# Raw weight words: the sign carried through the rebias by a leaky ReLU, and a new order of all work

## The chip, the cores and the metric

The kernel runs on one core of one Trainium2 chip. The metric is device time of one execution in microseconds (us), lower is better; a kernel's time is the median of its runs. The engines are called as in the profile: PE (matrix multiply; PEld is its weight load), DVE (vector), ACT (activations), POOL (general purpose) and SP (which issues the DMAs).

## The reference

Windowed attention (8 x 8 heads, 576 tokens, head size 64, window 64), whose result for all 4608 tokens goes through a gated feed-forward network with weights 512 x 2048 and 2048 x 512:

```python
scores = where(0 <= i - j < 64, q @ k.T / 8, -1e9)
attn   = softmax(scores)
x      = (attn @ v), heads side by side        # 4608 x 512
h      = x @ w_in                              # 4608 x 2048
g      = h * erf(softplus(h))
out    = g @ w_out                             # 4608 x 512
```

q, k and v are float32. The two weight matrices are drawn as float64, so that each weight reaches the kernel as two 32-bit words, a low and a high one.

## The kernel before, in words

**Attention.** Tokens are cut into 36 units of 128 (number u), two units to a chunk of 256 (number c, 18 chunks). Each unit's q, k and v are loaded (`lq`, `lk`, `lv`), their largest magnitudes found (`pk`) and turned into powers of two per chunk (`pa`, `pb`, `px`, `py`, `pc`). Every operand of a matrix product is split into two float16 parts, a high one (`qh`, `kh`, `vh`) and a rest (`ql`, `kl`, `vl`), and each product is three matmuls. Scores (`s`), masked maximum (`m`), shift (`f`), two exponentials (`e`), the rest of the weights (`r`), a transposing DMA (`t`), the weighing of v (`a`), normalization (`n`), the split of the result (`xh`, `xl`) and another transposing DMA into `xt` (`xt`) follow.

**Feed-forward.** A group g (36 of them) is one chunk with one half of the 2048 hidden columns. Its first product, `mm:g:0` to `mm:g:3` (24 matmuls each, PSUM tiles hp0 and hp1 in turn), needs `xt` of the chunk and both parts of `w_in`. Each piece is taken out of PSUM by an eviction `ev` on DVE or ACT into `h`; softplus (`sp`) and erf (`er`) run on ACT for half a group at a time, DVE multiplies (`gt`), `gh` and `gl` make the float16 parts, and `mA` (16 matmuls of 512 columns) and `mB` (8) form the second product in PSUM tiles o0 and o1, from where `fo` moves it to the result and `st` stores it. ACT holds one table of functions at a time: exponentials, softplus and erf each need their own, and the build puts an ACT_TABLE_LOAD wherever the next activation needs another one than the last.

**Weights.** They come in 16 units of 1 MB (`L`), eight of `w_in`, then eight of `w_out`, into six slots that are reused (`SLOTS`). A unit is 128 x 1024 pairs of words. For each unit the double is turned into a float32 in place: the high word, read as a float32, is multiplied by 2^-112 (`rebias`, token `c`); it is shifted left by 3 and joined with the low word's top three bits (`assemble`, token `o`, DVE). The shift pushes the sign out, so the sign is kept apart. Either `sign_plane` (token `g`, ACT or POOL) writes it into a tile `plane` and `low_bits` (`d`, DVE) joins the shifted low word with it, or `low_bits2` (`dd`, two DVE instructions) takes it from the high word. Then `b` (`bound`) finds the largest magnitude, `mb`, `mx`, `my`, `mc` make the scale of a pair of units, `h` writes the float16 high part, and `lp` on PE with `le` the rest (for two units `l` on DVE). `wm` tokens are matmuls on an identity whose result nobody reads; they run where PE has nothing else.

**Order.** `PLAN` is a list of 2356 tokens, written out in the file; each token calls the function of its name, and instructions stand on every engine's queue in the order of the tokens. The last letter names the engine (v DVE, a ACT, g POOL). Each engine works through its queue in order.

Of the kernel before, what the change touches and what calls it, by code (L numbers as in the profile page):

```python
# [8 lines left out]
F32 = mybir.dt.float32  # L9
# [28 lines left out]
SIGN = -(2 ** 31)  # L38
# [175 lines left out]
def window_attention_gated_ffn(ctx, tc, q, k, v, w_in, w_out, masks, out):  # L214
# [82 lines left out]
    for t in planes:  # L297
        nc.gpsimd.memset(t, 0)
# [185 lines left out]
    def low_bits(u):  # L484
        lo = raw(u)[0]
        nc.vector.scalar_tensor_tensor(lo, lo, 29, planes[u % len(planes)], op0=ALU.logical_shift_right, op1=ALU.bitwise_or)
# [225 lines left out]
```

## Time and profile before

| | |
|---|---|
| runs | 932.92 us median of 3 (929.71 to 935.45) |
| profiled execution | span 929.5 us, first to last instruction; no time of its own is given beside the span |
| PE | busy 897.9 us (97% of the span) |
| DVE | busy 714.7 us (77%) |
| ACT | busy 634.4 us (68%), in it 116 table loads |
| POOL | busy 290.8 us (31%) |
| DMA | 98.63 MB, mean 106 GB/s |

"Busy" of PE includes the `wm` matmuls. A group of instructions in the profile has a line (of the kernel), an engine, an operation, tiles written and read, a count, busy time and the mean of one in ns. Idle time is put down to what ended it.

### The profile page before, as it was taken

How to read it: one execution, taken by the hardware profiler on the slowest of the kernel's cores; microseconds unless marked ns; L12 is line 12 of the kernel's file. 1: busy time of each engine (PE TensorE's matmuls, PEld its weight loads, DVE VectorE, ACT ScalarE, POOL GpSimd, SP SyncE). 2: the span in 40 equal slices, each digit the busy share in tenths (PEclk: the TensorE clock that was granted, in tenths of full speed). 3: DMA queues.
4: the chain of work that ended last, by engine and by line, in shares of the span. 5: the costliest groups of instructions: out<-in, count | busy, mean ns of one | idle time of the engine just before them, and what ended most of it. 6: DMA issues, size and time to landing. Idle time of an engine off the chain costs nothing.

```text
span 929.5 us, 22240 instructions
## 1 busy us (share of the span) xinstructions
PE 897.9 (97%) x9281; PEld 603.5 (65%) x9281; DVE 714.7 (77%) x1506; ACT 634.4 (68%) x749; POOL 290.8 (31%) x299
## 2 busy tenths in 40 slices
PE   8779998999999999999999999999999999999998
PEld 8546566656766666667666767566667566766663
DVE  6989887988888998785976876986876976845443
ACT  4888976888675886959764758764768764924333
POOL 1343333425244353441330541330541430501000
PEclk9989999999999999999999999999999999999999
DMA  9585747144443555445353525352625250301000
GB/s 366 171 199 182 202 86 197 41 96 132 112 129 81 114 128 124 84 111 102 93 86 102 113 88 103 92 92 102 112 84 103 91 105 33 70 23 24 24 23 23
DMA packets 140532, 98.63 MB, mean 106 GB/s; under 512 B 117776, under 2 KB 117904, under 8 KB 140432
## 3 DMA queue, kind: packets, MB, share of 16 engines
q1 hardware_dynamic: 140432, 97.22, 42.2%
q8 instruction: 72, 1.18, 0.5%
q14 instruction: 28, 0.23, 0.1%
HBM read 59.44 MB, written 9.44 MB: 74 GB/s over the span
## 4 chain that ended last, share of the span: by engine, by line
PE 79%; DVE 10%; DMA 5%; ACT 3%; issue 1%; POOL 1%; DVEq 0%; POOLq 0%; ACTq 0%
PE hp L590 36%; PE o L626 35%; PE av L427 3%; PE s L394 2%; DMA vr<-v_in 2%; PE o L553 1%; DMA stage<-w_out 1%; DVE y L610 1%; DMA qr<-q_in 1%; DVE gl L322 1%; DMA xt<-xs 1%; DMA stage<-w_in 1%; DVE vs L322 1%; DVE sm L403 1%; DVE stage L504 1%
## 5 line engine op out<-in xcount | busy, mean ns | idle before, releaser
L590 PE MATMUL hp<-xt,w 128*128 128x256 f16 x3456 | 401.8, 274 | 7.8 <-DMA xt<-xs 3.6
L590 PEld LDWEIGHTS <-w 128*128 128x128 f16 x3456 | 336.7, 98 | 70.4 <-issue 11.4
L626 PE MATMUL o<-w,gh 128*128 128x512 f16 x1152 | 260.9, 379 | 2.5 <-DVE w L444 1.8
L626 PEld LDWEIGHTS <-gh 128*128 128x128 f16 x1152 | 110.3, 98 | 125.8 <-issue 2.4
L317 DVE TENSOR_SCALAR h<-hp,c 128x512 f32<-128x512 f32 x123 | 90.9, 745 | 79.4 <-PE hp L590 79.0
L626 PE MATMUL o<-w,gl 128*128 128x512 f16 x576 | 136.4, 380 | 0.0
L602 ACT ACTIVATE y<-h 128x1024 f32<-128x1024 f32 x72 | 73.6, 1052 | 91.3 <-DVE h L317 90.1
L408 POOL TENSOR_TENSOR sm<-sm,mx 128x512 f32<-128x512 f32 x66 | 71.7, 1099 | 105.8 <-DVE mx L403 105.5
L322 DVE SCALAR_TENSOR_TENSOR gl<-y,sg,gh 128x1024 f16<-128x1024 f32 x72 | 97.4, 1354 | 5.8 <-PE o L626 4.0
L610 DVE TENSOR_TENSOR y<-h,y 128x1024 f32<-128x1024 f32 x72 | 95.3, 1333 | 8.4 <-ACT y L606 8.2
L626 PEld LDWEIGHTS <-gl 128*128 128x128 f16 x576 | 54.1, 98 | 56.3 <-DVE gl L322 0.5
L450 POOL TENSOR_TENSOR xs<-x,xs 128x512 f16<-128x512 f32 x32 | 46.5, 1453 | 140.3 <-ACT xs L442 107.8
L606 ACT ACTIVATE y<-y 128x1024 f32<-128x1024 f32 x72 | 73.7, 1050 | 0.5
L403 DVE CUSTOM_DVE_ANT_0 sm<-s,mask 128x128 f32<-128x128 f32 x288 | 64.5, 285 | 9.9 <-PE s L394 5.2
L417 POOL TENSOR_TENSOR p<-sm,p 128x512 f16<-128x512 f32 x39 | 53.4, 1371 | 47.2 <-ACT sm L413 46.9
L412 ACT ACTIVATE p<-sm,shift,cde 128x512 f16<-128x512 f32 x72 | 58.1, 807 | 13.0 <-POOL sm L408 12.6
L315 ACT ACTIVATE gh<-y,sg 128x1024 f16<-128x1024 f32 x39 | 44.6, 1143 | 30.3 <-DVE y L610 26.3
L602 ACT ACT_TABLE_LOAD x47 | 60.3, 1283 | 0.8
L413 ACT ACTIVATE sm<-sm,shift,cde 128x512 f32<-128x512 f32 x72 | 58.6, 814 | 2.4
L319 POOL TENSOR_SCALAR vs<-vr,csc 128x1024 f16<-128x1024 f32 x28 | 34.6, 1237 | 78.8 <-PE av L427 67.7
L322 DVE SCALAR_TENSOR_TENSOR vs<-vr,csc,vs 128x1024 f16<-128x1024 f32 x36 | 52.5, 1462 | 6.3 <-POOL vs L319 5.9
L579 POOL TENSOR_SCALAR sg<-rw,csc,isw 128x2 f32<-128x2 f32 x33 | 17.9, 543 | 117.0 <-DVE cde L366 117.0
(140 smaller groups left out, 991.9 us busy)
## 6 DMA issues: line engine op xcount, KB each, us to landing
vr<-v_in SPq DMA_DIRECT2D x36, 512.0 KB, 4.4
kr<-k_in SPq DMA_DIRECT2D x36, 384.0 KB, 3.8
qr<-q_in SPq DMA_DIRECT2D x36, 256.0 KB, 2.8
out<-ob SPq DMA_DIRECT2D x36, 256.0 KB, 2.1
stage<-w_out SPq DMA_DIRECT2D x6, 1024.0 KB, 5.6
stage<-w_in SPq DMA_DIRECT2D x4, 1024.0 KB, 5.2
w<-w_in SPq DMA_DIRECT2D x2, 1024.0 KB, 11.0
w<-w_out SPq DMA_DIRECT2D x2, 1024.0 KB, 6.4
```

The lines of the kernel that those rows point to most:

```text
L317: nc.vector.tensor_scalar(dst, src, s, None, op0=ALU.mult)
L322: nc.vector.scalar_tensor_tensor(dst, src, s, hi, op0=ALU.mult, op1=ALU.subtract)
L403: nc.vector.tensor_tensor_reduce(smi(u, par)[:, j, :], sps[par][:, j, :], mask[:, var, :], 1.0, LOWEST, op0=ALU.add, op1=ALU.max, accum_ou ...
L408: eng_of(eng).tensor_tensor(s, s, m.unsqueeze(2).broadcast_to([P, HP, P]), op=ALU.subtract)
L412: nc.scalar.activation(pp[0][u % 2][:, HP * par:HP * par + HP, :], s, AF.Exp, bias=shift14, scale=es)
L413: nc.scalar.activation(s, s, AF.Exp, bias=shift14, scale=es)
L417: eng_of(eng).tensor_tensor(pp[1][u % 2][:, sl, :], smi(u, par), pp[0][u % 2][:, sl, :], op=ALU.subtract)
L590: nc.tensor.matmul(hps[pc % 2][:, f, :], w1[a][:, cc, fs], xt[b][c % 2][:, cc, :], start=(n == 0), stop=(n == 3 * NCC - 1))
L602: nc.scalar.activation(at(yb, g, n), at(hb, g, n), AF.Softplus)
L606: nc.scalar.activation(y, y, AF.Erf)
L610: nc.vector.tensor_tensor(y, at(hb, g, n), y, op=ALU.mult)
L626: nc.tensor.matmul(ops[j], a[:, f, ts], w2[b][:, hf * GF + f, :], start=f == 0 and a is gh and b == 0, stop=f == GF - 1 and a is gl)
```

## The change

**Words.** The high word times 2^-112 now goes through a parametric ReLU with slope -2^32, always on ACT. A positive word is scaled as before. A negative one becomes positive and its exponent grows by 32; the bit of value 32 in the exponent is the one that the shift by 3 moves into the sign place. So no sign is kept apart: `sign_plane`, `low_bits2` and the tile `plane` go, `low_bits` is one DVE shift for every unit, and `rebias` no longer runs on DVE or POOL.

```diff
-    def sign_plane(u, eng):
-        sgn = planes[u % len(planes)].bitcast(F16).rearrange("p (n w) -> p n w", w=2)[:, :, 1]
-        hi = raw(u)[1].bitcast(F32)
-        if eng == "g":
-            nc.gpsimd.tensor_scalar(sgn, hi, 2.0 ** -112, 1.0, op0=ALU.mult, op1=ALU.mult)
-        else:
-            nc.scalar.activation(sgn, hi, AF.Copy, scale=2.0 ** -112)
-
     def low_bits(u):
         lo = raw(u)[0]
-        nc.vector.scalar_tensor_tensor(lo, lo, 29, planes[u % len(planes)], op0=ALU.logical_shift_right, op1=ALU.bitwise_or)
-
-    def low_bits2(u):
-        lo, hi = raw(u)
         nc.vector.tensor_scalar(lo, lo, 29, None, op0=ALU.logical_shift_right)
-        nc.vector.scalar_tensor_tensor(lo, hi, SIGN, lo, op0=ALU.bitwise_and, op1=ALU.bitwise_or)
-
-    def rebias(u, eng):
+
+    def rebias(u):
         hf = raw(u)[1].bitcast(F32)
-        if eng == "g":
-            nc.gpsimd.tensor_scalar(hf, hf, 2.0 ** -112, 1.0, op0=ALU.mult, op1=ALU.mult)
-        elif eng == "v":
-            nc.vector.tensor_scalar(hf, hf, 2.0 ** -112, None, op0=ALU.mult)
-        else:
-            nc.scalar.activation(hf, hf, AF.Copy, scale=2.0 ** -112)
+        nc.scalar.activation(hf, hf, AF.Prelu, scale=2.0 ** -112, alpha=-2.0 ** 32)
```

**Order.** All of `PLAN` is written anew (2340 tokens). Its first line:

```diff
-    "wm:0:183 L:0 L:1 L:2 lq:0 L:3 L:4 lk:0 lm lq:1 lk:1 lv:1 lv:0 L:5 dd:0 c:0:g o:0 dd:1 b:0:a g:2:a c:1:v o:1 "
...
+    "L:1 L:0 lq:0 L:3 L:2 lk:0 L:5 lk:1 lq:1 lm wm:0:126 lv:1 lv:0 d:1 c:1 L:4 o:1 b:1:v c:0 d:0 pk:0:0:a o:0 b:0:a d:3 c:3 mb:0 mx:0 my:0 wm:1:19 "
...
```

Many tokens change their engine. Counted over the program: evictions `ev` on ACT 21 before and 49 now (on DVE 123 and 95); the largest magnitudes of k on ACT 8 and 19; `vh` on POOL 28 and 16, on ACT 5 and 12, on DVE 3 and 8; `f` on POOL 66 and 56, on DVE 6 and 16; `kh` on ACT 30 and 23. Table loads on ACT: 116 before, 171 now. The `wm` matmuls number 507 and 508.

**Place one: DVE's queue at the start of the program.** The stage tiles, w2 and y1 are the slots of the first raw units; acc holds their bounds. Before, the first rows are:

```order
L490 TENSOR_SCALAR stage0_149<-stage0_149 128x1024
L491 SCALAR_TENSOR_TENSOR stage0_149<-stage0_149 128x1024
L504 SCALAR_TENSOR_TENSOR stage0_149<-stage0_149 128x1024
L490 TENSOR_SCALAR stage1_150<-stage1_150 128x1024
L491 SCALAR_TENSOR_TENSOR stage1_150<-stage1_150 128x1024
L498 TENSOR_SCALAR stage1_150<-stage1_150 128x1024
L504 SCALAR_TENSOR_TENSOR stage1_150<-stage1_150 128x1024
L486 SCALAR_TENSOR_TENSOR w2_0_140<-w2_0_140,plane0_84 128x1024
L498 TENSOR_SCALAR w2_0_140<-w2_0_140 128x1024
```

L490 and L491 are `dd`, L498 is `c`, L504 is `o`, L486 is `d` with the plane. Now, from the same place:

```order
L475 TENSOR_SCALAR stage1_149<-stage1_149 128x1024
L483 SCALAR_TENSOR_TENSOR stage1_149<-stage1_149 128x1024
L491 TENSOR_REDUCE acc_63<-stage1_149 128x1
L475 TENSOR_SCALAR stage0_148<-stage0_148 128x1024
L483 SCALAR_TENSOR_TENSOR stage0_148<-stage0_148 128x1024
L475 TENSOR_SCALAR w2_1_140<-w2_1_140 128x1024
L498 TENSOR_REDUCE wtop_81<-av_152 1x1
```

A unit now has two conversion rows on DVE (L475 is `d`, L483 is `o`), three or four before; one bound (L491) moved here from ACT, and the pair's first scale (L498) stands behind two units where it stood behind four.

**Place two: ACT's queue in the middle of the program** (groups 16 and 17 before, 13 now). h is softplus's source, y its result and erf's; hp is the first product in PSUM. Before:

```order
L315 ACTIVATE ob0_148<-o0_156,sg_91 128x512
L315 ACTIVATE ob0_148<-o1_157,sg_91 128x512
L602 ACT_TABLE_LOAD
L602 ACTIVATE y0_144<-h0_142 128x1024 x2
L442 ACTIVATE xs0_0_130<-x0_129 128x512
L606 ACT_TABLE_LOAD
L606 ACTIVATE y0_144<-y0_144 128x1024 x2
L442 ACTIVATE xs0_1_131<-x0_129 128x512
L315 ACTIVATE gh_146<-y0_144,sg_91 128x1024
L602 ACT_TABLE_LOAD
L602 ACTIVATE y1_145<-h1_143 128x1024 x2
L606 ACT_TABLE_LOAD
```

L602 is softplus, L606 erf. Now (L581 is softplus, L585 erf, L409 and L410 the exponentials, L312 on hp an eviction):

```order
L581 ACT_TABLE_LOAD
L581 ACTIVATE y1_144<-h1_142 128x1024
L312 ACTIVATE h1_142<-hp0_153,c1_89 128x512
L585 ACT_TABLE_LOAD
L585 ACTIVATE y1_144<-y1_144 128x1024
L409 ACT_TABLE_LOAD
L409 ACTIVATE p0_0_120<-sm1_118,shift14_64,cde_78 128x512
L410 ACTIVATE sm1_118<-sm1_118,shift14_64,cde_78 128x512
L409 ACTIVATE p0_0_120<-sm0_117,shift14_64,cde_78 128x512
L410 ACTIVATE sm0_117<-sm0_117,shift14_64,cde_78 128x512
L312 ACTIVATE h1_142<-hp1_154,c1_89 128x512
L581 ACT_TABLE_LOAD
```

Two halves of a group shared a load of softplus and one of erf; now each half has its own pair, and evictions stand between.

More of the change, by code (lines that the diff above doesn't have):

```diff
@@ L37 @@
 LOWEST = -3.0e38
-SIGN = -(2 ** 31)
 EXP_BITS = 0x7F800000
@@ L249, in window_attention_gated_ffn @@
     ones = fixed("ones", [3, P], BF16)
-    planes = ring("plane", 1, [P, HE], I32)
     junk = fixed("junk", [P, HP * KW], mybir.dt.uint8)
@@ L296, in window_attention_gated_ffn @@
     nc.gpsimd.tensor_scalar(minus, unit, -1.0, 1.0, op0=ALU.mult, op1=ALU.mult)
-    for t in planes:
-        nc.gpsimd.memset(t, 0)
     for n in range(2):
@@ L651, in window_attention_gated_ffn @@
         "f": shift, "e": expo, "r": expo_rest, "t": turn, "a": weigh, "n": normalize, "xh": x_hi, "xl": x_lo,
-        "xt": x_turn, "L": fetch, "g": sign_plane, "d": low_bits, "dd": low_bits2, "c": rebias, "o": assemble,
+        "xt": x_turn, "L": fetch, "d": low_bits, "c": rebias, "o": assemble,
         "b": bound, "dg": pair_diag, "lp": low_sum, "le": low_out, "mb": pair_rows, "mx": pair_top, "my": pair_all, "mc": pair_scale, "h": high, "l": low,
```

324 rows, old and new, of the table PLAN are left out of this document.

## The prediction

> **What bounds the kernel now.** I read the shares of the engines first, then the busy time stage by stage, then what the chain of waits names in the early stages. The first row gives busy time, share and instruction count; the others give a stretch's length, then each engine's busy time in it, the granted PE clock and the DMA share.
>
> ```profile
> PE 897.9 (97%) x9281; PEld 603.5 (65%) x9281; DVE 714.7 (77%) x1506; ACT 634.4 (68%) x749; POOL 290.8 (31%) x299
> ```
> ```profile
> core 0: us, PE busy (x) PEld busy (x) DVE busy (x) ACT busy (x) POOL busy (x), PEclk, DMA share, GB/s
> 0.00:69.20 69.20, 54.64 (x736) 40.03 (x737) 55.51 (x120) 48.12 (x70) 23.35 (x33) 0.95 0.79 247
> 69.20:177.40 108.20, 97.53 (x1128) 71.60 (x1127) 92.02 (x224) 87.48 (x122) 35.89 (x35) 0.97 0.57 149
> 177.40:268.50 91.10, 89.66 (x891) 55.09 (x892) 81.18 (x172) 72.80 (x82) 43.46 (x38) 1.00 0.44 105
> 268.50:450.00 181.50, 180.95 (x1904) 121.15 (x1902) 147.38 (x320) 133.48 (x151) 66.41 (x65) 1.00 0.46 106
> 450.00:642.00 192.00, 191.49 (x1976) 128.44 (x1975) 149.24 (x321) 130.16 (x152) 61.84 (x70) 1.00 0.42 97
> 642.00:925.70 283.70, 283.67 (x2656) 187.17 (x2653) 188.58 (x352) 162.38 (x179) 59.86 (x60) 1.00 0.27 61
> 925.70:929.50 3.80, 0.00 (x0) 0.00 (x0) 0.75 (x1) 0.00 (x0) 0.00 (x0) 0.98 0.37 138
> ```
>
> I cut where the first `mm` begins (69.2), where `mA:1:0` begins (177.4), and where the plan reaches group 8 (268.5) and group 24 (642). Part of PE's busy time is the `wm` filling, here alone in the first two stretches:
>
> ```profile
> 0.00:69.20 69.20, 31.26 (x487) 29.27 (x487) 0.95 0.79 247
> 69.20:177.40 108.20, 1.39 (x20) 1.24 (x20) 0.97 0.57 149
> ```
>
> So PE lacks real work for 69.20 - 54.64 + 31.26 = **45.8 us** in the first stretch, 10.67 + 1.39 = **12.1** in the second, 1.4 in the third, 0.55 + 0.51 + 0.03 = 1.1 in the next three, and 3.8 behind its last matmul: 64.2 in all. The real matmuls are the same after the change. Everything it can gain lies in the first 58 us of that, and from 268.5 us on it can only lose.
>
> What is late there? The chain of waits (start, length, what) in the first two stretches, and the two waits of PE that follow from it:
>
> ```profile
> 45.45 4.20 DMA vr<-v_in
> 51.81 2.10 DVE stage L504
> 57.61 2.10 DVE w L486
> 151.19 6.86 DMA xt<-xs
> ```
> ```profile
> 129.52 4.78 PE L590 MATMUL hp<-xt,w 128*128 128x256 f16 x27 [2.01 <-ACT h L315]
> 158.09 5.13 PE L590 MATMUL hp<-xt,w 128*128 128x256 f16 x31 [3.56 <-DMA xt<-xs]
> ```
>
> Raw-word work on DVE (L504, L486) stands on the path between the first chunk's attention steps, and in the second stretch PE waits for an eviction on ACT and for the third chunk's `xt`. Both engines feeding PE are dense there (DVE 92.0, ACT 87.5 of 108.2).
>
> **The change, part by part.** Groups, with count, busy time and mean ns of one:
>
> ```profile
> L490 DVE TENSOR_SCALAR stage<-stage 128x1024 int32<-128x1024 int32 x6 | 4.2, 704 | 6.6 <-DMA stage<-w_in 6.0 <-DMA stage<-w_out 0.6
> L491 DVE SCALAR_TENSOR_TENSOR stage<-stage 128x1024 int32<-128x1024 int32 x6 | 7.4, 1227 | 0.2
> L486 DVE SCALAR_TENSOR_TENSOR stage<-stage,plane 128x1024 int32<-128x1024 int32 x4 | 5.7, 1430 | 0.0
> L498 DVE TENSOR_SCALAR w<-w 128x1024 f32<-128x1024 f32 x2 | 1.4, 688 | 0.0
> L500 ACT ACTIVATE stage<-stage 128x1024 f32<-128x1024 f32 x6 | 6.9, 1142 | 0.8 <-DVE stage L491 0.8
> L482 ACT ACTIVATE plane<-stage 128x1024 f16<-128x1024 f32 x3 | 4.1, 1362 | 0.6 <-DMA stage<-w_out 0.6
> L512 DVE TENSOR_REDUCE acc<-h 128x1 f32<-128x1024 f32 x1 | 1.2, 1204 | 0.0
> L417 DVE TENSOR_TENSOR p<-sm,p 128x512 f16<-128x512 f32 x33 | 29.3, 887 | 2.7 <-ACT sm L413 2.7
> L602 ACT ACTIVATE y<-h 128x1024 f32<-128x1024 f32 x72 | 73.6, 1052 | 91.3 <-DVE h L317 90.1 <-DVE gl L322 0.7
> ```
>
> *First stretch.* Ahead of the first `mm` the old plan has 3 `dd`, 7 `d` and 4 `c` on DVE: 3 x (0.704 + 1.227) + 7 x 1.43 + 4 x 0.69 = 18.6 us. The new one has 10 shifts of 0.704 = 7.0. One bound (1.20) and two `r` (0.89 each) come to DVE: net 11.6 - 3.0 = **8.6 us** less on the engine that was busy for 55.5 of 69.2. On ACT, 4 `c` and 5 `g` (4 x 1.14 + 5 x 1.36 = 11.4) become 10 `c` (11.4). The parametric ReLU itself stands in no row. By the nearest ones, 1.05 (softplus, same size) and 1.36 (the plane), its ten cost between 0.9 less and 2.2 more than at 1.14, the row of the copy that it replaces on the same words; I take that one. The new wait: every `o` on DVE now waits for ACT, where 4 of 10 units were scaled by DVE itself and one by POOL; behind it on DVE stand the next unit's `d` and the softmax steps of chunk 0, for which ACT and PE wait. At worst that is one ACT instruction for each of the five, 5.7, which leaves 2.9; if the vr and PE pieces of the chain carry it, only the d at 57.61 shrinks, by 1.4. So 1.4 to 8.6. I take **7**, near the upper end, since DVE had but 13.7 idle in the stretch and ACT gets nothing more. The DMAs hide behind it: the same bytes at a share of 0.79.
>
> For the next two steps, a piece of the chain with two `mm` (24 matmuls each), and the groups of evictions and table loads:
>
> ```profile
> 69.35 5.24 PE hp L590 x48
> ```
> ```profile
> L317 DVE TENSOR_SCALAR h<-hp,c 128x512 f32<-128x512 f32 x123 | 90.9, 745 | 79.4 <-PE hp L590 79.0
> L315 ACT ACTIVATE h<-hp,c 128x512 f32<-128x512 f32 x21 | 14.0, 678 | 12.0 <-PE hp L590 9.7 <-DVE y L610 2.3
> L602 ACT ACT_TABLE_LOAD x47 | 60.3, 1283 | 0.8
> L606 ACT ACT_TABLE_LOAD x41 | 52.6, 1283 | 0.7
> ```
>
> *Second stretch.* Four `dd` and two `d` (10.6) become six shifts (4.2), four evictions come to DVE from ACT (4 x 0.745 = 3.0), so DVE falls by 3.4 and ACT by 2.7. Two waits get cover. Between the last `xt` of chunk 2 and the first `mm` that reads it the old plan has only `s:6`; the new one has `mm:3:2`, half of the x48 row, 2.6 us of the 3.6 waited. Between `mm:2:0` and `mm:2:2`, which share hp0, the old plan has nothing; the new one has `s:5` and `mB:0:1`, against the 2.0 waited. That is 4.6, and about 1 more from the lighter queues. Against it, `mm:3:3` now follows `mm:3:1` on hp1 with little between them: up to 2.0 by the same wait. So 2.6 to 5.6, beyond that to 9 if the queues carry more of the 12.1; I take **5**.
>
> *From 177 us on.* The new plan has 55 more table loads, 55 x 1.283 = 70.6 us, and 28 more evictions on ACT, 28 x 0.678 = 19.0. In the third stretch there are 21 loads where 14 stood and 3 more evictions, over some 11 us more of PE's work: ACT goes from 80% (72.8 of 91.1) to about 90%. From group 8 to 24 there are 26 more loads and 29 more evictions, 33.4 + 19.7 = 53 us: ACT goes from (133.5 + 130.2) / 373.5 = 71% to 85%, while DVE loses 30 evictions (22 us) and takes shifts and splits from POOL in their place. PE's cover is the stock of finished groups between `mm` and `mA`. What it costs where the cover is thin: PE's one wait for an eviction in this stretch (waited us, times, longest):
>
> ```profile
> PE hp L590 <- DVE h L317: 0.5, 1, 0.5
> ```
>
> Places where the same hp tile is refilled after less than 2.7 us of PE's other work number 6 in the old plan and 18 in the new one. Twelve more at 0 to 0.5 are 0 to 6; I take 1.5, since most of the old ones cost nothing, and 1.5 (0 to 5) for the third stretch at 90%. Behind 642 us ACT has room (162.4 of 283.7).
>
> The loads are where a page speaks against this change:
>
> ```profile
> 497.76 2.00 ACT L602 ACTIVATE y<-h 128x1024 f32<-128x1024 f32 x2 [13.36 <-DVE h L317]
> 499.78 1.28 ACT L606 ACT_TABLE_LOAD   x1
> 501.07 1.06 ACT L606 ACTIVATE y<-y 128x1024 f32<-128x1024 f32 x1
> ```
>
> The load follows the last activation by 0.02 us and the next follows the load by 0.01: a switch costs 1.3 here. The Trainium skill, "ScalarE: Activation LUTs", section "What ACT_TABLE_LOAD costs", gives 1283 ns and a drain of 1380 ns behind it, 2.66 us for each switch, so that 55 more would be 146 us (an estimate from that page). The trace agrees with the 1283 and shows no drain.
>
> **Sum.** -7 - 5 + 1.5 + 1.5 = -9: a span of 920.5 after 929.5. The median of the runs lies 3.4 above the span, so 923.9, say **924**.
>
> **Rivals.**
> - *ACT takes DVE's place at the start.* Ten rebiases in one queue with the first chunk's scalings and exponentials: start 1.4, second stretch 2.6, behind it +4: 933. For it: ACT was already at 87.5 of 108.2. Against: its count there hardly moves. Chance 0.20.
> - *Slower: ACT paces the middle.* Place: groups 1 to 24. In the second stretch PE starved while ACT was used 81%. If the in-order queue can't be used more, the third stretch's 87 us on ACT need 107 for PE's 96 (+11), and 317 need 391 for 373.5 (+18): 932.9 - 12 + 29 = 950. It decides at 85%: with that much usable only the third stretch is late, +6, and the time is 927. For it: each half group now has its own pair of loads in its chain. Against: DVE had 81.2 of 91.1 (89%) in the third stretch with 1.4 us lost. Chance 0.11.
> - *More than I take.* DVE's whole 8.6, 9 of the 12.1, nothing lost behind: 915. Chance 0.12.
> - *A switch costs twice its row*, the load and as long again before the next activation. The 81 loads of groups 8 to 24 put 81 x 1.283 = 104 us more on ACT, 421 for 373.5: +47, 968. The three rows above leave no room for it; chance 0.02. The page just named has such a wait in its rule.
> - *It doesn't do what it says.* The new order shows no table load ahead of a rebias but the first, and no plane; nothing is left for this but the ReLU's duration, which is in the bounds.
>
> **How the numbers follow.** The forecast holds 0.55, between 917 and 932. A measurement of this kernel can tell about 1% from no change, 923.6 and 942.2. Half of the forecast's chance lies below 923.6: 0.28 + 0.12 = 0.40 faster. The other half and the first rival, 0.47, are within. Slower: 0.11 + 0.02 = 0.13. The range takes in the 915 case and the bounds (1.4 + 2.6 saved, 11 lost: 940): 911 to 940.
>
> **What would show it.** The first `mm` begins near 62 (69.2 before), with DVE near 47 busy ahead of it; `mA:1:0` near 165; PE idle between there and 642 us about 5. ACT near 720 busy with 171 loads of 1.283, the ReLU near 1.14. I am wrong if the first `mm` stays behind 67, or if PE waits for ACT's evictions or for `gh` more than 8 us behind group 1.

## The result, and the profile after

| | before | after |
|---|---|---|
| median of the runs | 932.84 us (929.71 to 935.45, 4 runs) | 942.82 us (941.06 to 943.90, 4 runs) |
| ratio to before | | 1.0106, 95% interval 1.0074 to 1.0138 |
| span of the profiled execution | 929.5 us | 941.8 us |

The change makes the kernel 1% slower; 924 was forecast and 911 to 940 given as the range. The span grew by 12.3 us where 9 less were expected. (The 3.4 us that the prediction added between span and time are 1.9 here: the profiled execution took 943.69.) The engines' totals after the change:

```profile
PE 906.7 (96%) x9282; PEld 606.3 (64%) x9282; DVE 701.2 (74%) x1533; ACT 724.5 (77%) x831; POOL 238.1 (25%) x231
```

ACT's 724.5 is what the prediction reckoned (720), and DVE has 13.5 less to do. The totals do not show where the time went; the stretches do. They are cut at the same events as before: the first `mm` (83.3), `mA:1:0` (185.2), group 8 (283.6), group 24 (650.6), with a cut at 450.

```profile
0.00:83.30 83.30, 63.65 (x759) 45.23 (x760) 49.33 (x118) 49.08 (x73) 10.66 (x25) 0.84 0.62 206
83.30:185.20 101.90, 94.67 (x1104) 69.08 (x1103) 85.29 (x220) 89.44 (x122) 37.61 (x33) 0.97 0.64 161
185.20:283.60 98.40, 98.11 (x942) 57.59 (x941) 85.10 (x182) 91.23 (x103) 16.45 (x16) 1.00 0.40 100
283.60:450.00 166.40, 165.65 (x1665) 112.58 (x1664) 126.97 (x284) 136.62 (x155) 33.77 (x33) 1.00 0.40 100
450.00:650.60 200.60, 197.72 (x2164) 132.64 (x2161) 165.79 (x377) 164.95 (x180) 64.55 (x58) 1.00 0.45 103
650.60:938.00 287.40, 286.87 (x2655) 189.13 (x2655) 188.00 (x355) 193.22 (x203) 75.09 (x66) 1.00 0.26 61
938.00:941.80 3.80, 0.00 (x0) 0.00 (x0) 0.75 (x1) 0.00 (x0) 0.00 (x0) 1.00 0.37 138
```

The largest loss is in the first row. The first `mm` begins at 83.3, 14.1 later than before. (The new order puts 13 `lp` tokens ahead of it where 12 stood; one is some 1.5 us of PE's work, an estimate from 17.7 us for the 12 before.) The second row wins 6.3 of it back (101.9 after 108.2), and the rows from 185.2 on lose 4.5 more. DVE's busy time ahead of the first `mm` fell as forecast, to 49.33 (47 forecast, 55.5 before), yet it is spread over 83 us: DVE stood still for 34 us. Its waits in that stretch (waited us, times, longest):

```profile
DVE kw L304 <- PE av L622: 12.5, 4, 5.2
DVE stage L475 <- DMA stage<-w_in: 5.9, 1, 5.9
DVE cpw L361 <- PE av L622: 5.4, 1, 5.4
DVE wtop L498 <- PE av L622: 2.9, 1, 2.9
```

L622 is the `wm` filling, whose results nobody reads; the rows on `kw`, `cpw` and `wtop` are the first instructions of `mc`, `pc` and `mx`. DVE waits 12.5 + 5.4 + 2.9 = **20.8 us** for it. In the same view of before, up to 69.2, the filling (L643) accounts for 1.9:

```profile
DVE den L432 <- PE av L643: 0.7, 1, 0.7
DVE kw L307 <- PE av L643: 0.6, 1, 0.6
DVE cpw L364 <- PE av L643: 0.6, 1, 0.6
```

One of these waits in order of time, PE first, then DVE:

```profile
48.98 0.17 PE L501 MATMUL av<-wtop,ones 1*128 1x1 bf16 x1
49.08 7.00 PE L622 MATMUL av<-ident 128*128 128x120 bf16 x128
```
```profile
50.29 0.67 DVE L475 TENSOR_SCALAR stage<-stage 128x1024 int32<-128x1024 int32 x1
56.12 0.16 DVE L304 TENSOR_SCALAR kw<-av 128x1 int32<-128x1 int32 x1 [5.15 <-PE av L622]
```

What the row on `kw` reads, one matmul (L501, token `my`), was there at 49.15. Behind it PE had 128 filling matmuls in its queue, which write another slice of the same PSUM tile `av`:

```python
crow, call = avb[:3, 0, row_at:row_at + P], avb[:, 0, row_at + P:row_at + P + 3]
wrow, wall = avb[:1, 1, row_at:row_at + P], avb[:, 1, row_at + P:row_at + P + 1]
idle = avb[:, 0, row_at + P + 3:row_at + P + 123]
```

It began 0.04 us after the last of them had ended. `mc` reads `wall` and `mx` reads `wrow`, both in the second half of `av` (index 1); `pc` reads `call` in the first half, where the filling (`idle`) writes. All three waited, so the wait does not need the same half. In the new `PLAN` such blocks stand between the matmul and its reader (`my:2 ... wm:6:128 ... mc:2`, `py:0 wm:4:71 pc:0`, `mb:2 wm:5:47 mx:2`, three more): six blocks with 365 matmuls. Before, six blocks stood so too, but with 140 matmuls. The chain of waits up to the first `mm` now goes through the filling for 28.3% (shares of its length):

```profile
by line: PE av L622 28.3%; PE o L532 21.2%; DMA stage<-w_in 6.2%; PE o L533 5.0%; PE av L424 3.2%; DVE stage L483 2.9%; ACT w L312 2.8%; issue 2.5%; PE s L391 2.5%; POOL sm L405 1.7%; ACT stage L489 1.5%; DVE acc L491 1.5%; DVE h L483 1.4%;
```

In the kernel before, the filling has 5.6% of that chain, some 3.9 us, most of them in one block, `wm:2:47` between `my:0` and `mc:0`. This piece stood in the profile before the change:

```profile
20.03 2.63 PE av L643 x47
```

### The profile page after: what moved, and what is told of

Its sections match the earlier page's. It is cut to its first block, busy times and chain, and to the rows that moved or that the text cites. A ratio compares the mean times of both kernels' runs of the same rounds, so it can differ in the third digit from the quotient of the medians.

```text
span 941.8 us, 22242 instructions
## 1 busy us (share of the span) xinstructions
PE 906.7 (96%) x9282; PEld 606.3 (64%) x9282; DVE 701.2 (74%) x1533; ACT 724.5 (77%) x831; POOL 238.1 (25%) x231
## 4 chain that ended last, share of the span: by engine, by line
PE 80%; ACT 7%; DVE 5%; DMA 5%; issue 1%; POOL 0%; SPq 0%; DVEq 0%; ACTq 0%
PE o L605 34%; PE hp L569 34%; PE av L424 3%; PE o L532 3%; PE av L622 3%; PE s L391 2%; DMA xt<-xs 2%; DMA vr<-v_in 1%; ACT y L581 1%; DMA stage<-w_out 1%; ACT L581 1%; ACT y L585 1%; ACT L585 1%; PE o L533 1%; DVE y L589 1%
## 5 line engine op out<-in xcount | busy, mean ns | idle before, releaser
L569 PE MATMUL hp<-xt,w 128*128 128x256 f16 x3456 | 397.3, 273 | 5.7 <-DMA xt<-xs 5.3
L405 POOL TENSOR_TENSOR sm<-sm,mx 128x512 f32<-128x512 f32 x56 | 69.4, 1244 | 204.0 <-DVE mx L400 203.9
L581 ACT ACTIVATE y<-h 128x1024 f32<-128x1024 f32 x72 | 75.8, 1056 | 53.4 <-DVE h L314 52.8
L589 DVE TENSOR_TENSOR y<-h,y 128x1024 f32<-128x1024 f32 x72 | 92.2, 1281 | 29.9 <-ACT y L585 29.7
L314 DVE TENSOR_SCALAR h<-hp,c 128x512 f32<-128x512 f32 x95 | 70.8, 746 | 42.0 <-PE hp L569 41.4
L585 ACT ACTIVATE y<-y 128x1024 f32<-128x1024 f32 x72 | 75.9, 1056 | 0.8
L414 POOL TENSOR_TENSOR p<-sm,p 128x512 f16<-128x512 f32 x36 | 47.8, 1329 | 93.1 <-ACT sm L410 93.0
L409 ACT ACTIVATE p<-sm,shift,cde 128x512 f16<-128x512 f32 x72 | 58.1, 807 | 15.4 <-POOL sm L405 12.1
L447 POOL TENSOR_TENSOR xs<-x,xs 128x512 f16<-128x512 f32 x26 | 36.3, 1397 | 96.9 <-ACT xs L439 59.4
L410 ACT ACTIVATE sm<-sm,shift,cde 128x512 f32<-128x512 f32 x72 | 58.6, 814 | 2.4
L319 DVE SCALAR_TENSOR_TENSOR vs<-vr,csc,vs 128x1024 f16<-128x1024 f32 x36 | 55.0, 1527 | 1.8 <-POOL vs L316 1.5
L312 ACT ACTIVATE gh<-y,sg 128x1024 f16<-128x1024 f32 x39 | 44.3, 1137 | 9.7 <-PE o L605 7.0
L312 ACT ACTIVATE h<-hp,c 128x512 f32<-128x512 f32 x49 | 33.1, 678 | 24.1 <-PE hp L569 24.1
```

What stands on the lines that cost most here:

```text
L312: nc.scalar.activation(dst, src, AF.Copy, scale=s)
L314: nc.vector.tensor_scalar(dst, src, s, None, op0=ALU.mult)
L319: nc.vector.scalar_tensor_tensor(dst, src, s, hi, op0=ALU.mult, op1=ALU.subtract)
L405: eng_of(eng).tensor_tensor(s, s, m.unsqueeze(2).broadcast_to([P, HP, P]), op=ALU.subtract)
L409: nc.scalar.activation(pp[0][u % 2][:, HP * par:HP * par + HP, :], s, AF.Exp, bias=shift14, scale=es)
L410: nc.scalar.activation(s, s, AF.Exp, bias=shift14, scale=es)
```

## The experiments

Theory A: DVE's readers wait for filling that is recorded between the matmul and them into the same tile. Rivals: B, the blocks delay PE's own queue, whoever reads; C, PE's granted clock, 0.84 in the first stretch after 0.95, makes the start slow. Besides, the word part may be at fault, or the order behind the start. Before, after and the twelve variants together; "first `mm`" and "`mA:1:0`" are when these begin, "last" is when the last matmul ends. All have done the same real matmuls at `mA:1:0` and at the last one. A ratio is taken against runs of before made alongside that variant, so it can differ a little from the quotient of the medians shown.

| kernel | first `mm` | `mA:1:0` | last | median us | ratio to before (95%) |
|---|---|---|---|---|---|
| before | 69.2 | 177.4 | 925.7 | 932.84 | |
| after | 83.3 | 185.2 | 938.0 | 942.82 | 1.0106 (1.0074 to 1.0138) |
| blocks behind their readers | 64.1 | 165.3 | 917.5 | 925.24 | 0.9928 (0.9902 to 0.9955) |
| filling left out but the first block | 66.7 | 167.0 | 918.9 | 922.43 | 0.9897 (0.9848 to 0.9947) |
| filling in another tile | 61.5 | 162.8 | 913.7 | 920.70 | 0.9884 (0.9847 to 0.9922) |
| one block behind its reader | 76.7 | 177.1 | 929.5 | 935.19 (one run) | |
| word part alone | 65.7 | 172.5 | 920.6 | 926.43 | 0.9940 (0.9916 to 0.9963) |
| word part, blocks behind readers | 71.1 | 178.7 | 927.9 | 931.66 | 0.9995 (0.9973 to 1.0017) |
| word part, filling in another tile | 63.9 | 170.0 | 918.9 | 923.45 | 0.9902 (0.9878 to 0.9926) |
| before, filling in another tile | 66.6 | 173.3 | 922.7 | 926.16 | 0.9931 (0.9902 to 0.9959) |
| old start, new order behind it | 71.0 | 177.3 | 937.3 | 943.12 | 1.0123 (1.0065 to 1.0181) |
| new start, old order behind it | 64.5 | 167.3 | 919.9 | 927.97 | 0.9952 (0.9937 to 0.9968) |
| other tile, old evictions from group 8 | 61.5 | 162.5 | 919.1 | 924.13 | 0.9915 (0.9896 to 0.9933) |
| other tile, new start, old order behind it | 61.4 | 161.3 | 912.5 | 919.81 | 0.9867 (0.9851 to 0.9883) |

**Blocks behind their readers.** Six tokens move in `PLAN`; no engine's queue changes, since `wm` is on PE and what it is moved past is not. Three of them (the others are `wm:5` behind `mx:2`, `wm:6` behind `mc:2` and `wm:7` behind `n:1`):

```diff
- my:0 wm:1:19 mc:0
+ my:0 mc:0 wm:1:19
...
- wm:3:52 le:1:0:a mc:1
+ le:1:0:a mc:1 wm:3:52
...
- py:0 L:8 wm:4:71 pc:0
+ py:0 L:8 pc:0 wm:4:71
...
```

> Six of the eight blocks of filling matmuls are moved in the plan, each from ahead of the DVE instruction that reads the little result which PE left in the tile `av` to just behind it. PE's queue and every other queue stay as they are, row by row; only what the readers wait for changes. Theory A (the readers wait for the whole block, since the fill writes the same tile): DVE's 20.8 us of waits for PE av in the first 83.3 us fall below 4, the first `mm` begins at 63 to 75 instead of 83.3, time 923 to 934. Theory B (PE works through the blocks ahead of the needed matmuls, in its queue, whoever reads): the blocks stand where they stood, the first `mm` stays at 80 to 84, time 940 to 944. Theory C (PE's lower granted clock, 0.86 and 0.80 at the start): the same as B.

925.24: A, and B and C fall. With the same 508 filling matmuls at the same places of PE's queue, the first `mm` begins 19.2 us earlier. DVE's waits there, the largest, hold no filling (L473 is `d`, L302 `kw`, L352 the chunk's maximum):

```profile
DVE stage L473 <- DMA stage<-w_in: 6.1, 1, 6.1
DVE kw L302 <- PE av L499: 1.6, 3, 1.2
DVE ctop L352 <- PE av L348: 1.5, 2, 1.1
```

The clock came back by itself, 0.97 in this row after 0.84, with the same matmuls: the low clock followed from PE's waiting:

```profile
0.00:64.09 64.09, 52.78 (x760) 39.95 (x761) 48.70 (x118) 48.31 (x72) 10.74 (x25) 0.97 0.81 267
```

But PE waits the other way round here: a filling matmul behind a reader waits until the reader is done with the tile.

```profile
PE av L620 <- DVE wtop L496: 2.5, 1, 2.5
PE av L620 <- DVE x L429: 1.5, 1, 1.5
PE av L620 <- DVE kw L302: 1.3, 3, 0.8
```

**Filling left out.** `wm:0:126` stays, 382 matmuls go.

```diff
- wm:1:19
...
- wm:2:17
...
- wm:3:52
...
- wm:4:71
...
- wm:5:47
...
- wm:6:128
...
- wm:7:48
```

> All blocks of filling matmuls but the first (126) are left out; 382 matmuls, some 24 us of PE's 33.4 us of filling, go, all real work stays in order. Theory A (readers wait for the block) and theory B (the block delays PE's own queue) both give a first `mm` at 62 to 72 and 922 to 932; together with the run in which the blocks only stand behind the readers this tells A from B. Theory C (the granted clock sets the start, and the filling holds it up): the clock falls below the 0.80 to 0.86 seen, the real matmuls of the start, some 30 us, take up to twice as long, and the first `mm` stays behind 80, time 938 to 960.

922.43, as A and B say, and not C's 938 to 960. Still, the clock does follow the filling:

```profile
0.00:66.70 66.70, 43.02 (x378) 23.10 (x378) 50.18 (x120) 49.81 (x74) 10.66 (x25) 0.72 0.76 258
```

0.72, where the kernel with all its filling and no wait for it (next) has 0.97, and a first `mm` 5.2 us later than there. The Trainium skill, "TensorE: Matmul & The Clock Gate", part 1 on the clock gate, says that the clock is held back by default and released by recent activity of PE; these two rows agree. The medians of the two kernels, 922.43 and 920.70, have intervals that overlap.

**Filling in another tile.** The order is that of the change, word for word.

```diff
-    idle = avb[:, 0, row_at + P + 3:row_at + P + 123]
     hps = [ps.tile([P, 2, CT], F32, name=f"hp{i}") for i in range(2)]
+    idle = hps[0][:, 0, :120]
```

> The changed kernel with its order untouched; only the target of the filling matmuls is another PSUM tile (hp0, not in use before the first `mm`) and no longer a slice of `av`. If a reader waits for the block because the block writes the tile that it reads: the waits on the filling go, DVE's 20.8 us fall below 4 in the first stretch, first `mm` at 63 to 68, time 923 to 929, as with the blocks behind the readers (925.2). If the reader waits because PE reports only the last matmul ahead of it in the program, whatever tile that writes: first `mm` at 80 to 84, time 940 to 944.

920.70, below the 923 to 929 expected, with the first `mm` at 61.5. One line's change of address takes 22 us off the changed kernel: the wait comes from the shared tile, not from how far PE's queue has got. A part of the 22 came by way of the clock that fell with the waits: PE spent some 30 us on real matmuls ahead of the first `mm` in the changed kernel (63.65 less 33.41 of filling) and some 22 here (53.71 less 31.54). Neither engine waits for the other on the filling's account, except for the identity at the start:

```profile
0.00:61.47 61.47, 53.71 (x760) 40.45 (x760) 48.39 (x118) 48.00 (x72) 10.73 (x25) 0.97 0.86 278
```
```profile
PE hp L622 <- POOL ident masks.py:199: 1.8, 1, 1.8
```

**One block.** Only `wm:4:71` goes behind `pc:0`.

```diff
- py:0 L:8 wm:4:71 pc:0
+ py:0 L:8 pc:0 wm:4:71
```

> The changed kernel with one block alone moved behind its reader: the 71 matmuls between `py:0` and `pc:0`, for which DVE waited 5.4 us. If the waits stand one behind another on the chain: first `mm` at 77.5 to 79, span 936 to 937. If another wait takes over at once: first `mm` at 82 to 83, span 940 to 942.

The span is 933.3, 8.5 less, and the first `mm` 6.6 earlier, slightly more than the 5.4 waited and more than both cases allowed: this wait stood on the chain and passed on in full, in the one execution there is. The 11.9 for `kw` are still there.

```profile
DVE kw L302 <- PE av L620: 11.9, 4, 5.2
```

**The word part alone.** Before's `PLAN` with `dd` written `d`, `c` without an engine, and no `g`; the new word functions.

```diff
-    "wm:0:183 L:0 L:1 L:2 lq:0 L:3 L:4 lk:0 lm lq:1 lk:1 lv:1 lv:0 L:5 dd:0 c:0:g o:0 dd:1 b:0:a g:2:a c:1:v o:1 "
+    "wm:0:183 L:0 L:1 L:2 lq:0 L:3 L:4 lk:0 lm lq:1 lk:1 lv:1 lv:0 L:5 d:0 c:0 o:0 d:1 b:0:a c:1 o:1 "
```

> The word part alone: the order of before, with every rebias as a parametric ReLU on ACT, one DVE shift for each unit and no sign planes. The prediction's reckoning (DVE has up to 11.6 us less to do ahead of the first `mm`): first `mm` at 62 to 68, time 923 to 932. Rival (the words wait for ACT, which becomes the late engine at the start): first `mm` at 69 to 75, time 932 to 940. If the fault of the change lies in the word part and not in the order: first `mm` near 80, time above 940.

926.43, as the prediction's reckoning had it. The parametric ReLU is not at fault. DVE's busy time ahead of the first `mm` is 46.5 and ACT's 47.6 (55.5 and 48.1 before):

```profile
0.00:65.74 65.74, 54.34 (x736) 40.18 (x737) 46.50 (x114) 47.60 (x70) 16.70 (x29) 0.95 0.81 260
```

**The word part, blocks behind readers.** Six blocks move, PE's queue stays. Three of them (the others are `wm:1` behind `mx:0`, `wm:3` behind `mx:1`, `wm:12` behind `n:1`):

```diff
- my:0 wm:2:47 b:2:a d:4 pk:0:1:a mc:0
+ my:0 b:2:a d:4 pk:0:1:a mc:0 wm:2:47
...
- py:0 wm:5:9 L:6 pc:0
+ py:0 L:6 pc:0 wm:5:9
...
- wm:11:11 dg:2 n:0
+ dg:2 n:0 wm:11:11
```

> The word part with the order of before (926.4), and six of its blocks of filling matmuls moved behind the DVE instruction whose operand they would cover; all queues stay as they are. DVE waited 4.3 us for filling there ahead of the first `mm` (2.0, 1.2, 0.6, 0.5). If waits for filling pass on to the first `mm` as they did with the new order: first `mm` at 62 to 64, time 922 to 925. If these small ones are covered by other work: 925 to 928.

A miss: 931.66, slower than without the move. DVE no longer waits for filling, but PE now waits for DVE ahead of it, 7.0 us, and the real matmuls behind the filling come later (first `mm` 71.1 after 65.7):

```profile
PE av L620 <- DVE wtop L496: 4.0, 2, 3.6
PE av L620 <- DVE x L429: 3.0, 2, 1.8
```

Within one tile the filling cost on one side or the other; the move won with the new order and lost with this one.

**The word part, and the kernel before, with the filling in the other tile.** The address as above in both; `wm:13:6` and `wm:14:14`, which stand behind the first `mm`, are left out.

```diff
-    idle = avb[:, 0, row_at + P + 3:row_at + P + 123]
+    idle = hps[0][:, 0, :120]
...
- wm:13:6
...
- wm:14:14
```

> The word part with the order of before, the filling in hp0 (without its last two blocks). DVE's 4.3 us of waits for filling go, and no block can wait for a reader, as the blocks moved behind readers did (PE waited 7.0 us for DVE ahead of filling there, which gave 931.7). First `mm` at 61.5 to 64 after 65.7, time 922 to 925. If the waits for filling were covered: as the word part alone, 925 to 928.

> The kernel before, unchanged but for the target of its filling matmuls: hp0 in place of `av`; its last two blocks (20 matmuls, behind the first `mm`) are left out since hp0 is in use there. In before DVE waited 1.9 us for filling ahead of the first `mm` (0.7, 0.6, 0.6) and PE waited for nothing there on its filling's account but the identity at the start. If only waits that the profile shows count: 929 to 932. If before too hides more behind the shared tile: 925 to 928.

923.45 and 926.16. The first is as expected. The second falls under the second of its cases: the kernel before gains about 6 us from another tile (0.7%, interval 0.4 to 1.0%), though DVE's three waits sum to 1.9. The profiled execution shows less, a span 3.0 shorter (926.5), with the first `mm` 2.6 and `mA:1:0` 4.1 earlier:

```profile
0.00:66.58 66.58, 53.04 (x735) 39.20 (x736) 55.65 (x120) 47.93 (x70) 25.84 (x33) 0.97 0.82 257
66.58:173.25 106.67, 96.77 (x1107) 70.30 (x1106) 92.97 (x224) 87.41 (x121) 37.57 (x35) 0.97 0.57 152
```

The 2.6 fit the chain better than the sum of DVE's waits: the filling had some 3.9 us of the chain up to the first `mm`. The 1.5 won in the second stretch may be no more than the 20 matmuls left out there, which took 1.4. The profiled execution was one of the longer ones (928.74), so how much of the 6 is the tile is open.

**Old start, new order behind it; and the reverse.** Each kernel takes one order up to `mA:1:0` and from there the other's order for all work not yet done.

```diff
  e:6:1 gh:1:1:v
- mA:1:0 gl:1:0 t:6:0 gl:1:1 sp:3:0 r:6:1:v mB:1:0
+ vh:6:v vl:6 lv:8 pk:8:2:v gn:5:g r:6:1:g gn:7:v t:6:0 r:6:0:v mA:1:0 gl:1:0 t:6:1 sp:3:0 mB:1:0
```

> The old kernel and its order up to `mA:1:0`, from there the new order (with the old word functions for the last units). If the new order behind that point costs by itself what the two traces differ by there (4.5 us; 3 were predicted): 935 to 939. If that difference is only an after-effect of the late start: 930 to 934. In both cases the first `mm` stands at 69 to 70 and PE reaches `mA:1:0` near 177.

> The new order with the blocks behind the readers up to `mA:1:0` (PE without real work for 46.4 us there), then the order of before. If the parts add (before loses 8.0 us from there on, the run with the blocks behind the readers 11.8): span 917, time 918 to 922. If the seam costs a wait of its own, as it did in the other splice (one of 6.0 us for `gl`): 924 to 930.

943.12, above both of its ranges, and 927.97, in the range for a seam that waits. Both seams cost a wait of their own, so neither measures the late part by itself:

```profile
PE o L627 <- DVE gl L323: 6.0, 1, 6.0
```
```profile
PE o L603 <- DVE gl L317: 5.1, 1, 5.1
```

From `mA:1:0` to the last matmul the first takes 760.0 (before 748.3, the change 752.8): 6.0 of the 11.7 more is the seam; the rest was not followed.

**Old evictions from group 8 on,** with the filling in the other tile: 29 `ev` tokens from ACT back to DVE, for example

```diff
- ev:8:0:a
+ ev:8:0:v
...
- ev:8:3:a
+ ev:8:3:v
```

> The changed kernel with the filling in hp0 (920.7), and from group 8 on all 29 evictions that the new order gave to ACT back on DVE. If ACT's evictions cost what PE loses more behind group 8 than in before (10.3 against 5.3 us of lost time): 915 to 918. If not: 919 to 924, and more if DVE then becomes late.

924.13 after 920.70: no gain; from `mA:1:0` to the last matmul it takes 756.7 where the same order with ACT's evictions takes 750.9. Back on DVE they saved nothing, so ACT's evictions were not what cost time there.

**New start, old order behind it, other tile,** joined behind `mB:1:1`, so that `l:14` does not stand ahead of `gl`.

```diff
  a:6:1 mB:1:1 pk:9:2:v
- gh:2:1:a ev:5:0:v ev:5:1:a pa:4 mm:5:2
+ dg:7 sp:3:1 gh:2:1:a er:3:1 r:7:0:g ev:5:0:v fo:1:1 mm:5:2
```

> The new order with the filling in hp0 up to `mB:1:1`, then the order of before; the row at the seam for which PE waited 5.1 us in the last splice (`gl` behind a low part of the weights on DVE) stays where the new order has it. If the late part of the old order is better by what the traces show (4 to 5 us): 914 to 918. If the seam waits again: 919 to 926.

919.81, the lowest median here, without the wait for `gl`. It is 1.3% faster than before, but against the 920.70 of the change with one line altered the intervals overlap. From `mA:1:0` on it takes 751.1, no less than the new order's 750.9, so the 4 to 5 us expected of the old order did not come. The join was not free either: 10 us behind it PE waits for the normalization (`x`), a wait that neither of the two orders has by itself:

```profile
PE av L348 <- DVE x L429: 2.4, 1, 2.4
```

## Why the prediction was wrong

**The first stretch, -7, is the step that failed**: +14.1 at the first `mm` came in its place. Its inner working held. DVE has 49.33 busy there (47 forecast); the rebiases on ACT cost what was taken, the parametric ReLU 1.153 against 1.14, and the wait of `o` for ACT is small (1.6 in the row below and 0.7 for the tile `y`, where 5.7 was taken at worst):

```profile
L479 ACT ACTIVATE stage<-stage 128x1024 f32<-128x1024 f32 x10 | 11.5, 1153 | 8.3 <-DMA stage<-w_in 5.3 <-DMA stage<-w_out 3.0
L483 DVE SCALAR_TENSOR_TENSOR stage<-stage 128x1024 int32<-128x1024 int32 x10 | 12.2, 1220 | 1.7 <-ACT stage L479 1.6
```

What it left out is the filling. The prediction subtracted `wm` from PE's busy time as work that fills gaps, and gave its new places no price. Six of eight blocks stand between a result and its reader in one tile, with 365 matmuls where 140 stood so before, and that is 19 to 22 us (83.3 to 64.1 or to 61.5). With the filling in another tile, the first stretch measures 7.7 us less than before. But 2.6 of that the same edit gives to before: like with like, 66.6 to 61.5, it is -5.1 for the -7, with 1.5 more real work in it.

**The second stretch, -5, was right in size.** It takes 101.9 (108.2 before); less the 1.5 of real work that lies ahead of it now, -4.8. The ways were partly others. The wait for an eviction went, as forecast. The one for `xt` fell only from 3.6 to 3.0, not by 2.6, and the one for a bound on ACT (L510 before, L489 now) grew from 1.0 to 3.1. The first row is before's, the others are the change's:

```profile
PE av L516 <- ACT stage L510: 1.0, 1, 1.0
```
```profile
PE av L495 <- ACT stage L489: 3.1, 1, 3.1
PE hp L569 <- DMA xt<-xs: 3.0, 2, 1.6
PE av L358 <- DVE cdiag L355: 0.8, 1, 0.8
```

The waits that the prediction did not name, for `w` and `qs` on DVE, went too.

**From 177 us on, +3, was near**: 752.8 from `mA:1:0` to the last matmul, 748.3 before, +4.5; with the filling in the other tile +2.6, and +1.4 against before with the same edit (749.5 and 750.9). But not where it was put. PE's waits from 185.2 to 650.6, the largest; 0.3 us of them are for ACT's evictions:

```profile
PE hp L569 <- DMA xt<-xs: 2.2, 2, 1.5
PE o L605 <- DVE ob L614: 0.6, 1, 0.6
PE av L358 <- DVE cdiag L355: 0.5, 1, 0.5
PE hp L569 <- ACT h L312: 0.3, 1, 0.3
```

The third stretch lost 0.3 us, not the 2.9 forecast (1.4 and 1.5 more). From group 8 to 24 PE lost 3.6 where it had lost 1.1, 2.6 more for the 1.5 put there, but the largest wait is for `xt`, not for an eviction. Another part lies in PE's busy time: the groups of PE's instructions behind `mA:1:0` have the same 1440 matmuls of the attention's weighing of v, before and after,

```profile
L427 PE MATMUL av<-vs,pt 128*64 128x65 f16 x1440 | 29.9, 197 | 0.3 <-DVE cpw L364 0.3
```
```profile
L424 PE MATMUL av<-vs,pt 128*64 128x65 f16 x1440 | 32.7, 197 | 0.3 <-DVE cpw L361 0.3
```

which cover 2.8 us more at the same mean of 197 ns, that is, they overlap less. It goes with the order: with the old order behind `mB:1:1` this row has 30.2. Why was not settled.

**Luck in the sum.** With the filling in the other tile on both sides, the three parts are -5.1, -5.3 and +1.4: the span falls by 9.0 (926.5 to 917.5), the forecast -9. That is partly luck: the parts were sized -7, -5 and +3, their mechanisms hold only in part, and the medians differ by 5.5.

**The rivals.** ACT as the new engine at the start: no, it waits for DMAs there (L479 above). "ACT paces the middle": no; ACT was used for 91.23 of 98.4 us in the third stretch, 93%, beyond the 85% from which that rival was to decide, and PE lost 0.3. A doubled price of a table switch: no. Behind 151 of the 171 loads of 1.28 the next activation begins within 0.02; behind the other 20 it waits for an operand from DVE, POOL or a DMA:

```profile
533.04 1.28 ACT L581 ACT_TABLE_LOAD   x1
534.33 1.06 ACT L581 ACTIVATE y<-h 128x1024 f32<-128x1024 f32 x1
```

No rival named the filling, the slower ones all had ACT as their engine, and even the upper end of the range (940) counted 1.4 saved in the first stretch; it ended 2.8 us short. The condition "wrong if the first `mm` stays behind 67" was the right alarm, for a reason that the prediction did not have.

**What the change is worth** with the filling in a tile of its own: before 926.16, the word part 923.45, the whole change 920.70. Steps of about 3 us are within the intervals, and even for the two ends, 0.9931 and 0.9884, the intervals still meet (between 0.9902 and 0.9922).

## What to carry to other kernels

Let filling work on PE write a tile that nobody reads meanwhile. In these kernels a reader of another slice of a shared tile waited for all the filling recorded ahead of it, and filling behind a reader made PE wait in turn. When an order is rewritten, look for each filler between a result and its reader, and search the chain and the waits of the other engines for the filler's line, however small its share was before (1.9 us of waits, 5.6% of the chain). Price every token that moves, those whose result nobody needs as well.

## What was not expected of the hardware

- The granted clock follows how densely PE is fed, not the number of filling matmuls alone: 0.84 over the first stretch with 508 of them and DVE waiting 20.8 us for them, 0.97 with the same 508 and no such wait, 0.72 with 126.
- ACT can be busy for 93% of a stretch of 98.4 us, with 22 table loads in it, and PE still loses only 0.3 us.
- A parametric ReLU on 128 x 1024 words takes 1.12 to 1.15 us, as the plain scaling did (1.14), and only the first of them has a table load ahead of it.
